# First block of a transformer kernel: modulated and projected in halves of 256 queries, with the first loads reordered and the later ones held back

## The chip, the cores and the metric

The kernel runs on one core of a Trainium2 chip. The metric is device time in microseconds (us) of one execution. Before the change it is 564.21 us, the median of 3 runs (564.14 to 564.25). All runs told here are of state "fast" (none is over 1.5% above the fastest of its kernel); comparisons are between runs of the same rounds on the same chip, unless it is said that runs of two groups are taken together.

## The reference

A layer norm with modulation from a vector c, grouped attention over the last 512 keys, a projection, and a second modulated norm with an MLP. Only the beginning matters here:

```python
mod = (_silu(c) @ w_mod).reshape(c.shape[0], 6, 1, -1)     # c: (1, 512), w_mod: (512, 3072)
sa, ca, ga, sb, cb, gb = ...
h = _layernorm(x) * (1 + ca) + sa                          # x: (1, 2048, 512), bf16
q = h @ wq                                                 # 32 heads of 128
scores = einsum('bhqd,bhkd->bhqk', q, k) * Dh ** -0.5      # k: last 512 rows of the cache
# ... softmax, @ v, @ wo; x + ga * A; second norm with sb, cb; MLP; x + gb * B
```

## The kernel before

Five engines work side by side: TensorE (PE; its weight loads are PEld), VectorE (DVE), ScalarE (ACT), GpSimd (POOL) and SyncE (SP), which here only issues loads. The 2048 queries go through in four blocks of 512. A block has four tiles of 128 rows (xn). They are normalised, transposed into hT (features on partitions), modulated on the way out of PSUM (the memory that TensorE writes to), and multiplied with wq one head at a time. The kernel starts with the loads; `eng=ACT` issues on ScalarE's queue, everything else on SyncE's:

```python
    for i in range(2):
        dma(x_sb[:, 2 * i:2 * i + 2, :], xv[:, 2 * i:2 * i + 2, :], f"xa{i}", writes=R_x[2 * i:2 * i + 2], eng=ACT if i else SP)
    dma(c_row[:, :], c[0].rearrange("(c p) -> c p", p=P), "c", writes=[R_c])
    load_wm01(0)            # first half of the modulation weights, 512 KB
    load_wm01(1, ACT)       # second half
    load_wq(0, 2, ACT)
    load_wq(2, 2)
    load_k(0)
    load_v(0)
    # ... constants
    warm(7)                 # 512-column matmuls on ones; their result is not used
    silu_exp(5)             # transposes c and takes its exp
    warm(9)
    # ... statistics of tile 3 on ACT
    ln_stat(0); ln_stat(1); rstd_add(0, 2); rstd_pow(0, 2)
    ln_stat(2); rstd_add(2, 3); rstd_pow(2, 4)
    silu_mul(5)             # rest of SiLU, on DVE
    for tl in range(3):
        ln_norm(tl)         # DVE
    # ... norm of tile 3 on ACT
    fs = mod_cols_mm(0, QBK)            # 32 one-column matmuls with wm0 and wm1
    # ... first half of fs, transposes of tile 0, second half of fs
    mod_cols_evac(0, QBK)
    for tl in range(1, TPB):
        ln_tposes(tl, [0, 2])
        warm(tl)
    ln_mod_ps([0, 2], hT[0], R_hT[0], 1)   # modulation, 512 columns a piece: two on DVE, two on ACT
    # ... further loads
    q_mms(0)
    q_mms(1, 5)
```

(Commands on one line are put together here; cuts are marked.)

## Time and profile before

| | before |
|---|---|
| time, span | 564.26, 562.5 us |
| x landed (two halves) | 4.78, 4.98 us |
| modulation weights landed (ACT half, SP half) | 6.16, 7.95 us |
| 32 modulation columns begin | 8.25 us |
| first modulation (hT) | 10.80 us |
| first score matmul | 13.47 us |

The rows below the first are from the start of the span and tell when each stage begins. PE is the bound for the rest of the span, so a change of the start is worth what it moves the first score matmul. The lines are in the prediction. The clock column of a stretch tells the granted TensorE clock as the trace's clock records have it; before the first record it reads 1.00, while the matmuls of that time take the 0.43 us of half speed. In this profile the record begins at 6.72.

### The profile page before, as it was taken

Reading aid. Unit: us, or ns where it says so; the run is one execution under the profiler, and the core shown is the slowest. Engines: PE = TensorE matmul, PEld = TensorE weight load, DVE = VectorE, ACT = ScalarE, POOL = GpSimd, SP = SyncE. Lnnn points to the kernel's source line nnn. Section 1 sums busy time; section 2 is a strip of 40 time slices with the busy share of each in tenths; the row PEclk is TensorE's granted clock in tenths of the full one; section 3 lists DMA queues with packets and bytes.
Section 4 is the critical chain, followed back from the end, with each engine's and each line's share of the span. In section 5 each row is a group of like instructions: output and inputs, shape, how many; then the busy total and the mean of one; then the engine's idle time right before and its main releaser. Section 6 shows DMA issues by size and latency. Waiting matters only on the chain.

```text
span 562.5 us, 9700 instructions
## 1 busy us (share of the span) xinstructions
PE 553.7 (98%) x4097; PEld 316.9 (56%) x4172; DVE 242.2 (43%) x533; ACT 350.4 (62%) x453; POOL 38.7 (7%) x42
## 2 busy tenths in 40 slices
PE   8999999999999999999999999999999999999998
PEld 3565555555555555555555555555555654444444
DVE  4444465533334655333346553333354448321134
ACT  5986666666666666666666666666666644432500
POOL 1000000003300000033000000330000000000000
PEclk9999999999999999999999999999999999999999
DMA  9778776421331247332523522121123220210001
GB/s 268 204 165 167 143 160 132 113 38 38 39 76 37 39 93 133 57 94 46 144 56 57 102 50 39 39 40 40 39 39 72 44 31 0 41 36 24 22 28 48
DMA packets 113310, 42.70 MB, mean 76 GB/s; under 512 B 93928, under 2 KB 112104, under 8 KB 113256
## 3 DMA queue, kind: packets, MB, share of 16 engines
q1 hardware_dynamic: 112024, 40.82, 35.2%
q10 hardware_dynamic: 1232, 1.15, 0.6%
q8 instruction: 35, 0.57, 0.5%
q14 instruction: 19, 0.16, 0.1%
HBM read 18.35 MB, written 2.10 MB: 36 GB/s over the span
## 4 chain that ended last, share of the span: by engine, by line
PE 97%; issue 1%; DMA 1%; DVE 1%
PE psS L1363 28%; PE psO L1363 26%; PE psQ L1363 23%; PE psW L1363 20%; DMA x<-in_A_x_dram 1%; DVE st L1373 0%; PE psS L1366 0%; DVE mv L1374 0%; DVE rstd L1574 0%; DVE PT L1673 0%; DVE PT L1675 0%; DVE tmp L1427 0%; DVE sc_bf L1428 0%; DVE tmp L1426 0%
## 5 line engine op out<-in xcount | busy, mean ns | idle before, releaser
L1482 ACT ACTIVATE PT<-psS 128x1024 bf16<-128x1024 f32 x256 | 262.6, 1028 | 129.5 <-PE psS L1363 129.4
L1363 PE MATMUL psS<-qT,kT 128*128 128x512 bf16 x509 | 151.1, 379 | 0.2
L1363 PEld LDWEIGHTS psO<-v,PT 128*128 128x128 bf16 x2048 | 126.6, 98 | 30.2
L1363 PE MATMUL psO<-v,PT 128*128 128x129 bf16 x2048 | 137.0, 220 | 0.0
L1363 PE MATMUL psQ<-hT,wq 128*128 128x512 bf16 x507 | 130.3, 379 | 0.1
L1492 DVE RECIPROCAL rinv<-psO 128x4 f32<-128x4 f32 x128 | 23.4, 183 | 233.1 <-PE psO L1363 233.1
L1363 PE MATMUL psW<-wo,oT 128*128 128x512 bf16 x451 | 117.9, 379 | 3.2
L1493 DVE TENSOR_TENSOR o<-psO,rinv 128x512 bf16<-128x512 f32 x128 | 88.5, 692 | 4.4
L1363 PEld LDWEIGHTS psQ<-hT,wq 128*128 128x128 bf16 x508 | 49.6, 98 | 60.7 <-issue 0.5
L1363 PEld LDWEIGHTS psS<-qT,kT 128*128 128x128 bf16 x512 | 49.6, 98 | 59.3 <-ACT PT L1482 0.7
L1474 ACT ACTIVATE qT<-psQ 128x512 bf16<-128x512 f32 x127 | 75.2, 592 | 0.5 <-PE psQ L1363 0.5
L1662 ACT ACTIVATE wq<-psS 128x512 bf16<-128x512 f32 x56 | 33.4, 597 | 49.6 <-PE psS L1363 49.6
L1363 PEld LDWEIGHTS psW<-wo,oT 128*128 128x128 bf16 x512 | 45.0, 98 | 32.9 <-DVE acc L1515 1.2
L1515 DVE TENSOR_TENSOR acc<-psW,acc 128x512 f32<-128x512 f32 x48 | 33.2, 691 | 6.7 <-PE psW L1363 6.7
L1363 PE MATMUL psO<-wmw,wq 128*128 128x512 bf16 (+1 forms) x164 | 32.7, 352 | 0.3
L1518 POOL TENSOR_TENSOR acc<-acc,gaf 128x512 f32<-128x512 f32 x12 | 15.3, 1272 | 168.7 <-DVE acc L1515 168.7
L1379 POOL TENSOR_TENSOR rstd<-rstd,cst 128x4 f32<-128x4 f32 x7 | 7.1, 1012 | 265.3 <-DVE rstd L1378 265.3
L1363 PE MATMUL psS<-h2T,wmw 128*128 128x512 bf16 x110 | 25.2, 379 | 0.1
L1673 DVE TENSOR_TENSOR PT<-psO,gbf 128x512 f32<-128x512 f32 (+1 forms) x12 | 7.5, 624 | 40.4 <-PE psO L1363 40.4
L1363 PEld LDWEIGHTS psO<-wmw,wq 128*128 128x128 bf16 x168 | 15.4, 98 | 16.5
L1363 PE MATMUL psS<-hT,wmw 128*128 128x512 bf16 x110 | 24.4, 379 | 0.1
L1373 DVE BATCH_NORM_STATS2 st<-x 128x6 f32<-128x512 bf16 x31 | 21.0, 678 | 4.8 <-DMA x<-in_A_x_dram 4.8
(73 smaller groups left out, 170.4 us busy)
## 6 DMA issues: line engine op xcount, KB each, us to landing
wo<-in_A_wo_dram SPq DMA_DIRECT2D x4, 1024.0 KB, 5.7
wq<-in_A_wq_dram SPq DMA_DIRECT2D x7, 512.0 KB, 5.7
wmw<-in_B_w_dram SPq DMA_DIRECT2D x14, 256.0 KB, 3.3
wmw<-in_w_mod_dram SPq DMA_DIRECT2D x5, 512.0 KB, 4.7
oT<-o SPq DMA_TRANSPOSE x128, 2.4
out_dram<-PT SPq DMA_DIRECT2D x15, 128.0 KB, 1.8
x<-in_A_x_dram SPq DMA_DIRECT2D x3, 512.0 KB, 4.1
v<-in_A_v_cache_dram SPq DMA_DIRECT2D x8, 128.0 KB, 4.8
```

What stands on the lines that cost most here:

```text
L1363: kb.op(PE, lambda e: e.matmul(out_ap, lhsT, rhs, start=start, stop=stop), reads=reads, group_writes=[R_b[k] for k in bk], signal=signal)
L1373: kb.op(DVE, lambda e: e.bn_stats(st[:, t, :], x_sb[:, t, :]), reads=[R_x[t]], writes=[R_st[t]])
L1379: kb.op(POOL, lambda e: e.tensor_tensor(rstd[:, sl], rstd[:, sl], cst[:, 0:1].to_broadcast([P, hi - lo]), op=ALU.pow), reads=R_rstd[sl] + ...
L1474: kb.op(ACT, lambda e: e.activation(qT[u % NQT][:, :], bank[bk], ACTF.Copy), reads=[R_b[bk]], writes=[R_qT[u % NQT]])
L1482: kb.op(ACT, lambda e: e.activation(PT[u % NPT][:, pr * 2:pr * 2 + 2, :], s_ps[pr][:, :, :], ACTF.Exp, scale=scale), reads=[R_b[pr * 2], R ...
L1492: kb.op(DVE, lambda e: e.reciprocal(rinv[:, u, :], o_ps[:, :, P]), reads=[R_b[5], R_b[6]], writes=[R_rinv])
L1493: kb.op(DVE, lambda e: e.tensor_tensor(o_sb[u % NOS][:, :, :], o_ps[:, :, 0:P], rinv[:, u, :].unsqueeze(2).to_broadcast([P, TPB, P]), op=A ...
L1515: kb.op(DVE, lambda e: e.tensor_tensor(acc[:, tl, :], bank[WBK], acc[:, tl, :], op=ALU.add), reads=[R_b[WBK], R_acc[tl]], writes=[R_acc[tl]])
L1518: kb.op(eng, lambda e: e.tensor_tensor(acc[:, tl, :], acc[:, tl, :], gaf[:, :], op=ALU.mult), reads=[R_acc[tl], R_ga], writes=[R_acc[tl]])
L1662: kb.op(ACT, lambda e: e.activation(h1T[b % 2][:, fc, :], bank[bk], ACTF.Relu), reads=[R_b[bk]], writes=[R_h1[b % 2][fc]], pre=all_events( ...
L1673: kb.op(DVE, lambda e: e.tensor_tensor(yt[i][:, c0:c1], bank[bk][:, c0:c1], gbf[:, c0:c1], op=ALU.mult), reads=[R_b[bk], R_gb], writes=[R_ ...
```

## The change

It wants to bring the first score matmul forward in four ways: the SiLU of c off the chain behind the statistics (c loaded first), fewer loads in flight until x has landed, tile 3 normalised on POOL, and the first block modulated and projected in two halves of 256 queries, so that the second half's norms and transposes lie beside the first half's modulation.

```diff
+    dma(c_row[:, :], c[0].rearrange("(c p) -> c p", p=P), "c", writes=[R_c], eng=ACT)
     for i in range(2):
         dma(x_sb[:, 2 * i:2 * i + 2, :], xv[:, 2 * i:2 * i + 2, :], f"xa{i}", writes=R_x[2 * i:2 * i + 2], eng=ACT if i else SP)
-    dma(c_row[:, :], c[0].rearrange("(c p) -> c p", p=P), "c", writes=[R_c])
     load_wm01(0)
     load_wm01(1, ACT)
-    load_wq(0, 2, ACT)
+    kb.op(SP, lambda e: e.nop(), reads=[R_x[0]])
+    load_wq(0, 2)
+    load_k(0)
     load_wq(2, 2)
-    load_k(0)
     load_v(0)
 ...
-    warm(7)
+    warm(6)
     silu_exp(5)
-    warm(9)
+    warm(8)
 ...
+    silu_mul(5)
     ln_stat(0)
 ...
-    silu_mul(5)
-    for tl in range(3):
-        ln_norm(tl)
- ...  (tile 3 on ACT)
+    ln_norm(0)
+    ln_norm(1)
+    kb.op(POOL, lambda e: e.tensor_scalar(xn[:, t3, :], x_sb[:, t3, :], s3[:, 1:2], rstd[:, t3:t3 + 1], op0=ALU.add, op1=ALU.mult), ...)
 ...
+    ln_tposes(0, TB[0])
+    ln_tposes(1, TB[0])
+    warm(1)
+    mod_half(0, 0, DVE)
+    mod_half(0, 2, ACT)
+    mod_half(0, 1, DVE)
+    mod_half(0, 3, ACT)
+    ln_norm(2)
+    q_half(0, 0, CC_ORDER[:3], QBK)
+    ln_tposes(3, TB[1])
+    ln_tposes(2, TB[1])
+    q_half(0, 0, CC_ORDER[3:], QBK)
+    mod_half(1, 0, DVE)
+    mod_half(1, 2, ACT)
+    mod_half(1, 1, DVE)
+    mod_half(1, 3, DVE)
+    q_half(1, 0, CC_ORDER, 5)
+    for u, bk in ((0, QBK), (1, 5)):
+        q_half(u, 1, CC_ORDER, bk)
+        q_evac(u, bk)
 ...
-    q_mms(0)
-    q_mms(1, 5)
```

More of the change, by code (lines that the diff above doesn't have):

```diff
@@ L1311, in build_fast @@
     R_st, R_mv, R_rstd = RL("st", NT), RL("mv", NT), RL("rstd", NT)
+    R_h0 = RL("h0", DC)
     R_s3, R_eps = Res("s3"), Res("eps")
@@ L1397, in ln_tposes @@
         for cc in range(DC):
-            bk = bks[cc // 2]
+            bk = bks[cc]
             o = (cc % 2) * 512 + tl * P
             tpose(bank[bk].bitcast(BF)[:, o:o + P], xn[:, tl, cc * P:(cc + 1) * P], [R_xn[tl]], [bk], cc == DC - 1)
-    def ln_mod_ps(bks, dst, R_dst, which):
-        o, r = (0, R_moda) if which == 1 else (2 * DC, R_modb)
-        for k in range(2):
-            for half, eng in ((0, DVE), (1, ACT)):
-                cc = half * 2 + k
-                src = bank[bks[half]].bitcast(BF)[:, k * 512:(k + 1) * 512]
-                sc, sh = modc[:, o + DC + cc:o + DC + cc + 1], modc[:, o + cc:o + cc + 1]
-                if eng is DVE:
-                    kb.op(DVE, lambda e, src=src, sc=sc, sh=sh, cc=cc: e.tensor_scalar(dst[:, cc, :], src, sc, sh, op0=ALU.mult, op1=ALU.add),
-                          reads=[R_b[bks[half]], r], writes=[R_dst[cc]])
-                else:
-                    kb.op(ACT, lambda e, src=src, sc=sc, sh=sh, cc=cc: e.activation(dst[:, cc, :], src, ACTF.Identity, bias=sh, scale=sc),
-                          reads=[R_b[bks[half]], r], writes=[R_dst[cc]])
     CC_ORDER = (0, 2, 1, 3)
@@ L1469, in q_mms, with q_evac @@
         b, h = units[u]
-        order = CC_ORDER if u < QA else range(DC)
-        for i, cc in enumerate(order):
+        for i, cc in enumerate(range(DC)):
             mm(bank[bk], wq_sb[:, cc, h * Dh:(h + 1) * Dh], hT[b % 2][:, cc, :], i == 0, i == DC - 1,
-               [R_wq[h], R_hT[b % 2][cc]], [bk], i == DC - 1)
+               [R_wq[h], R_hT[b % 2][cc]] + ([R_h0[cc]] if b == 0 else []), [bk], i == DC - 1)
+        q_evac(u, bk)
+    def q_evac(u, bk=QBK):
         kb.op(ACT, lambda e: e.activation(qT[u % NQT][:, :], bank[bk], ACTF.Copy), reads=[R_b[bk]], writes=[R_qT[u % NQT]])
@@ L1586, in build_fast @@
     rstd_pow(2, 4)
-    silu_mul(5)
-    for tl in range(3):
-        ln_norm(tl)
-    kb.op(ACT, lambda e: e.activation(s3[:, 3:4], s3[:, 1:2], ACTF.Copy, scale=rstd[:, t3:t3 + 1]), reads=[R_s3, R_rstd[t3]], writes=[R_s3])
-    kb.op(ACT, lambda e: e.activation(xn[:, t3, :], x_sb[:, t3, :], ACTF.Identity, scale=rstd[:, t3:t3 + 1], bias=s3[:, 3:4]),
-          reads=[R_x[t3], R_rstd[t3], R_s3], writes=[R_xn[t3]])
-    fs = mod_cols_mm(0, QBK)
-    for f in fs[:len(fs) // 2]:
-        f()
-    ln_tposes(0, [0, 2])
@@ L1597, in build_fast @@
-    for f in fs[len(fs) // 2:]:
+    ln_norm(0)
+    ln_norm(1)
+    kb.op(POOL, lambda e: e.tensor_scalar(xn[:, t3, :], x_sb[:, t3, :], s3[:, 1:2], rstd[:, t3:t3 + 1], op0=ALU.add, op1=ALU.mult),
+          reads=[R_x[t3], R_rstd[t3], R_s3], writes=[R_xn[t3]])
+    for f in mod_cols_mm(0, QBK):
         f()
     mod_cols_evac(0, QBK)
-    for tl in range(1, TPB):
-        ln_tposes(tl, [0, 2])
-        warm(tl)
-    ln_mod_ps([0, 2], hT[0], R_hT[0], 1)
+    HB = QB // 2
+    R_half = [R_h0, R_hT[0]]
@@ new lines, in build_fast, with mod_half @@
+    TB = [[0, 0, 2, 2], [1, 1, 3, 6]]
+    def mod_half(hf, cc, eng):
+        bk = TB[hf][cc]
+        o = (cc % 2) * 512 + hf * HB
+        src, dst = bank[bk].bitcast(BF)[:, o:o + HB], hT[0][:, cc, hf * HB:(hf + 1) * HB]
+        sc, sh = modc[:, DC + cc:DC + cc + 1], modc[:, cc:cc + 1]
+        if eng is DVE:
+            kb.op(DVE, lambda e: e.tensor_scalar(dst, src, sc, sh, op0=ALU.mult, op1=ALU.add), reads=[R_b[bk], R_moda], writes=[R_half[hf][cc]])
+        else:
+            kb.op(ACT, lambda e: e.activation(dst, src, ACTF.Identity, bias=sh, scale=sc), reads=[R_b[bk], R_moda], writes=[R_half[hf][cc]])
@@ new lines, in q_half @@
+    def q_half(u, hf, order, bk):
+        for cc in order:
+            mm(bank[bk][:, hf * HB:(hf + 1) * HB], wq_sb[:, cc, u * Dh:(u + 1) * Dh], hT[0][:, cc, hf * HB:(hf + 1) * HB], cc == CC_ORDER[0], cc == CC_ORDER[-1],
+               [R_wq[u], R_half[hf][cc]], [bk], cc == CC_ORDER[-1])
+    ln_tposes(0, TB[0])
[7 more added lines that the diff above has]
+    q_half(0, 0, CC_ORDER[:3], QBK)
@@ L1604, in build_fast @@
+    ln_tposes(3, TB[1])
[8 more added lines that the diff above has]
+        q_half(u, 1, CC_ORDER, bk)
+        q_evac(u, bk)
     load_wq(R, R)
```

## The prediction

> **What bounds the kernel now.** I read the page first: its busy shares, then its chain that ended last.
>
> ```profile
> span 562.5 us, 9700 instructions
> PE 553.7 (98%) x4097; PEld 316.9 (56%) x4172; DVE 242.2 (43%) x533; ACT 350.4 (62%) x453; POOL 38.7 (7%) x42
> ...
> PE 97%; issue 1%; DMA 1%; DVE 1%
> ```
>
> TensorE (PE) is busy 98% and is 97% of the chain. DMA, DVE and issue are 3% of the chain between them, and the change works only on those and on the matmuls just behind them. Next I cut the span into stretches (columns: stretch, length, busy us of each engine with its instructions, clock, DMA share, GB/s).
>
> ```profile
> 0.00:4.80 4.80, 3.44 (x9) 1.12 (x10) 0.00 (x1) 1.54 (x3) 1.02 (x9) 1.00 0.59 191
> ...
> 300.00:400.00 100.00, 99.21 (x786) 59.43 (x799) 42.87 (x99) 69.02 (x86) 11.74 (x10) 1.00 0.27 48
> ```
>
> From 300 to 400 us PE has under 1 us in 100 to give away, and the change leaves that work as it is. Whatever it brings must come from the start, before the first score matmul (psS<-qT,kT). PE is "busy" there too, but with matmuls on a tile of ones that only keep its clock up. So for the start I read the chain of waits, in order of time (start, length, what).
>
> ```profile
> 0.79 3.99 DMA x<-in_A_x_dram
> ...
> 4.80 0.70 DVE st L1373
> ...
> 7.71 0.09 DVE tmp L1426
> ...
> 7.82 0.19 DVE tmp L1427
> ...
> 8.03 0.17 DVE sc_bf L1428
> ...
> 8.25 0.55 PE psQ L1363 x16
> ...
> 10.11 0.43 PE psW L1363 x2
> 10.54 0.22 PE psS L1366 x4
> ```
>
> The reader is to see three stages. Until 4.80 all wait for the first half of x. From there to 8.2 DVE does the statistics of three tiles and then the SiLU of c (tmp, sc_bf), which the modulation matmuls wait for. From 8.25 PE does modulation columns, transposes and, in between, clock-keeping matmuls. The timeline has the end of the start (start, length, engine, operation, what ended the idle time).
>
> ```profile
> 10.80 1.45 ACT L1413 ACTIVATE hT<-psS,modc 128x512 bf16<-128x512 bf16 x2 [1.08 <-PE psS L1366]
> 10.80 1.00 DVE L1410 TENSOR_SCALAR hT<-psS,modc 128x512 bf16<-128x512 bf16 x2 [0.98 <-PE psS L1366]
> ...
> 12.73 0.60 ACT L1474 ACTIVATE qT<-psQ 128x512 bf16<-128x512 f32 x1 [0.48 <-PE psQ L1363]
> ...
> 13.47 0.59 PE L1363 MATMUL psS<-qT,kT 128*128 128x512 bf16 x2
> ```
>
> The first score matmul is at 13.47. If later work only shifts, the time changes by as much as this number does. Last, the DMA issues of the first 3 us (size, us from issue to landing):
>
> ```profile
> wmw<-in_w_mod_dram SPq DMA_DIRECT2D x1, 512.0 KB, 6.3
> wq<-in_A_wq_dram ACTq DMA_DIRECT2D x1, 256.0 KB, 7.4
> ...
> kT<-in_A_k_cache_dram SPq DMA_TRANSPOSE x1, 7.2
> ```
>
> With issue times 1.65, 1.71 and 2.62 from the timeline, they land at 7.95, 9.1 and 9.8. The wq half is not used before 11.5, kT not before 13.4: both are early by some us, which lets them be held back.
>
> **What the Trainium skill says.**
> - "DMA: Bandwidth & Descriptors", section "Issuing engines are not separate DMA queues": transfers from different issuers run on the same 16 DMA engines and interleave; "Queues, rings and completion order" adds that each engine takes turns between queues. The trace agrees in part: between 3 and 4.5 us the ACT queue takes 79% and the SP queue 23% of the engines. But in that stretch only 40 packets are under 2 KB: x and the modulation weights have 2 KB rows, wq has 512-byte rows. So wq, kT and v, which the change holds back, had hardly begun when x landed. What still shares with x is what the change leaves in flight.
> - "TensorE: Matmul & The Clock Gate", section "The HAM clock gate": half clock until about 3.4 us of sustained activity. The trace agrees: 512-column matmuls issue every 0.43 us until 6.7 and every 0.22 afterwards.
> - "GPSIMD Engine Reference", section "Elementwise — side-by-side cycle accounting": a tight loop takes 769 ns for 512 elements, two-input operations more. No row here is a one-input POOL operation of that size; the two-input one (acc times gaf, 128x512) takes 1272 ns. My estimate for the new POOL operation is 0.95 us, between them.
> - "VectorE: DVE Perf Modes", section "The perf-mode tier table": a tensor_scalar that reads PSUM reaches at most twice the basic rate. The two modulations start 0.46 us apart for 512 columns, under the 0.53 that one element per cycle at its 0.96 GHz would need, so that rate is in use.
>
> **The change part by part.** I rebuild the start with durations from this trace, and with the new instruction order and waits from the built program.
>
> *1. SiLU ahead of the statistics; c first on the ACT queue.* c leaves at 0.78 instead of 1.24, with no x in front of it in its queue. It should land by 3 instead of 4.5. Six clock-keeping matmuls of 0.43 from 1.04 end at 3.6, then the transpose of c (0.18), exp (0.17) and three DVE operations (pitch 0.2) end near 4.6. So 0.49 us (7.62 to 8.11) leaves the DVE chain behind the statistics and lies in time in which DVE idled. DVE is free for the statistics from about 4.55.
>
> *2. Less in flight.* x's first half goes alone for about 0.4 us, because c delays the second. By the packet sizes the rest buys little. I choose a landing at 4.4 (before: 4.8), so the statistics start at S = 4.55, 0.25 earlier. The second half lands at about 4.9 as before; its first DVE use is S + 1.8 = 6.4, so it is in time.
>
> *3. Norms and modulation columns.* From the statistics' start to the end of the last rstd addition is 2.9 us (4.80 to 7.70). Then two norms (pitch 0.32, last one 0.41) end at S + 3.55 = 8.1. PE does its eight clock-keeping matmuls (3.75 to about 7.0), then the 32 modulation columns (16 take 0.38 to 0.55) once both weight halves have landed. The SP half is issued 0.45 earlier with no wq behind it: 7.0 to 7.3. So they end near 8.0, where they used to begin at 8.25. The DVE copies of the columns (2 x 0.2) end near 8.45; transposes of tiles 0 and 1 end (0.22 each and 0.2 to drain) near 8.6. The first modulation starts at T = 8.65, not 10.80.
>
> *4. Halves.* A 256-column modulation: from 4 and 512 columns (162 and 542 ns on DVE) about 0.35; on ACT from 1 and 512 columns (294 and 773 ns) about 0.53. Half 0, two each: DVE done at 9.3, ACT at 9.65. The norm of tile 2 follows on DVE, 9.65. POOL: power 7.5 to 8.25, then tile 3 until 9.2. PE: three query matmuls of 0.11 behind the modulations, tile 3 from 9.45, tile 2 from 9.7, drained at 10.15. Half 1: DVE does three in a row, 10.15 to 11.1; ACT's one is hidden. The last query matmul and drain (0.3) end at 11.4, the copy (0.6) at 12.0, the score matmul follows 0.15 later: 12.15 to 12.3.
>
> So 13.47 becomes about 12.25, a gain of 1.2 us. Two 256-wide operations cost more than one 512-wide one (0.70 against 0.54 on DVE), and three serial ones sit on the path; but they replace 1.45 us on ACT, and two clock-keeping matmuls (0.43 at 10.11) and the third tile leave the path.
>
> *5. What is held back.* SP waits for x (4.4), then issues wq (0.5), kT (1.2 to 1.8), the other wq and v. Weights drain until about 6.5, wq (256 KB at the 340 GB/s of this stretch: 0.8) lands near 7.7, needed at 9.0; kT near 9.5, needed at 12.2; the second wq near 10.7, needed at 12.7. All in time, the tightest by 1.3 us.
>
> *Sum:* 564.21 - 1.2 = 563.0 us, 0.2% less.
>
> **The rivals.**
> - *The held-back loads become the wait.* For it: kT took 7.2 us to land; at 5.0 + 7.2 = 12.2 it would be exactly on the edge. Against: its 7.2 had 1.5 MB in front of it; here most of that is gone by 6.5. If true, the gain shrinks to 0 to 0.8: 563.4 to 564.2.
> - *POOL or DVE sets the end.* If tile 3 takes 1.6 us on POOL rather than 0.95, its transposes move to 9.9 and the gain falls by 0.2; beyond that one for one. ACT's old version ended at 9.72. Time: 563.2 to 563.6.
> - *The clock.* PE has more gaps between 8.6 and 12 than before (two fillers are gone). A return to half speed for one window would cost about 1 to 2 us: 564 to 565. Against: my estimate still has PE busy some 65% there.
> - *x lands much earlier.* Then SiLU, not x, starts the statistics at 4.55, so no more than 0.1 comes of it.
> - *The gain is swallowed later.* ACT is busy 11.2 of the 11.6 us after 13.44, but that work begins with the first scores, so it shifts too. I see no fixed-time event behind it.
>
> **Range and chances.** The clear terms are SiLU and the fillers (0.5 and 0.4); the landing of x, POOL's time and the DMA edge each leave 0.2 to 0.5 open. I take 562.5 to 563.8. For 2% the time would have to change by 11.3 us, near the length of the whole start, so "within 2%" is almost certain: 0.98, with 0.01 each for the others.
>
> **What would show it.** Right: exp of c before 4.2 and sc_bf before x's first statistics; x landing 4.2 to 4.6; first hT at 8.4 to 8.9; first score matmul at 12.1 to 12.5; PE waits of no DMA after x but perhaps w_mod; the stretch from 300 to 400 unchanged. Wrong: PE waiting for wq or kT; POOL's tile 3 over 1.3 us; 512-column matmuls 0.43 apart after 8 us; or a first score matmul that moved by more or less than the total did.

## The result and the profile after

The changed kernel takes 565.35 us (median of 6 runs, 563.86 to 566.50); the kernel before took 564.12 in the same rounds (6 runs). The ratio is 1.0021, with a 95% interval of 1.0007 to 1.0036: within 2%, but slower, and above the predicted range of 562.5 to 563.8. A ratio here is the mean time of one kernel's runs over that of the other's of the same rounds, so it is not quite the ratio of the medians.

The page of the changed kernel, span, busy shares and chain:

```profile
span 563.1 us, 9781 instructions
PE 557.5 (99%) x4173; PEld 318.0 (56%) x4173; DVE 243.0 (43%) x536; ACT 349.5 (62%) x452; POOL 39.4 (7%) x43
...
PE 98%; DMA 1%; DVE 0%; ACTq 0%; issue 0%; ACT 0%
```

PE is the bound as before. The page alone hides where the time went: a busier PE looks better. (PE's records went from 4097 to 4173: the trace of before lacks some matmuls, so its 98% is a little low.) The chain of waits of the changed kernel's start (start, length, what):

```profile
0.79 0.56 ACTq L1298
...
1.39 0.37 ACTq L1298
...
1.79 6.37 DMA wmw<-in_w_mod_dram
...
8.21 0.90 PE psQ L1364 x30
...
9.62 0.42 DVE hT L1595
```

Before, the chain went through x, the statistics and SiLU. Now it goes through one load: the second half of the modulation weights (wmw), issued at 1.79 as third on ACT's queue and landed at 8.16. Statistics, norms and SiLU are off the chain, as intended, but what took their place is nearly as late: the columns begin at 8.21, where they began at 8.25. The timeline at the same places (start, length, engine, what; in brackets the idle time and what ended it):

```profile
4.63 0.68 DVE L1374 BATCH_NORM_STATS2 st<-x 128x6 f32<-128x512 bf16 x1
...
6.28 0.63 ACT L1558 ACTIVATE xn<-x 128x512 bf16<-128x512 bf16 x1 [2.17 <-DMA x<-in_A_x_dram]
...
8.21 0.90 PE L1364 MATMUL psQ<-sc_bf,wmw 128*128 128x1 bf16 x30 [1.13 <-DMA wmw<-in_w_mod_dram]
...
9.37 0.77 POOL L1580 TENSOR_SCALAR xn<-x,s,rstd 128x512 bf16<-128x512 bf16 x1
...
14.20 0.59 PE L1364 MATMUL psS<-qT,kT 128*128 128x512 bf16 x2 [0.34 <-ACT qT L1463]
```

PE idles 1.13 us for the weights, ACT 2.17 us for the second half of x. The first modulation is at 9.62 (before 10.80), 1.2 us earlier, yet the first score matmul comes at 14.20 (before 13.47). So between them the changed kernel needs 4.58 us where my prediction had 3.6. The stretches tell why. Columns are stretch, length, busy us of PE, PEld, DVE, ACT and POOL, clock, DMA share, GB/s; after, then before:

```profile
6.12:9.53 3.41, 2.23 (x45) 1.48 (x42) 2.25 (x9) 2.04 (x6) 1.57 (x3) 1.00 1.25 260
9.53:12.94 3.41, 3.16 (x20) 2.21 (x19) 2.12 (x7) 1.59 (x3) 0.61 (x1) 0.50 1.20 297
12.94:16.36 3.42, 3.08 (x18) 1.41 (x16) 0.31 (x1) 2.62 (x5) 0.00 (x0) 1.00 1.12 330
300.00:400.00 100.00, 100.00 (x808) 59.66 (x806) 43.54 (x101) 69.44 (x87) 11.73 (x10) 1.00 0.28 50
```

```profile
6.72:10.13 3.41, 2.88 (x50) 1.97 (x50) 2.62 (x11) 1.48 (x4) 1.48 (x2) 1.00 1.30 248
10.13:13.54 3.41, 3.33 (x18) 1.31 (x17) 1.33 (x3) 2.04 (x3) 0.00 (x0) 1.00 1.16 322
```

From 9.53 to 12.94, exactly in the tail of transposes and query matmuls, the granted clock is 0.50; before, it stays at 1.00. "PE busy 3.16" is not work done there: the same matmuls take twice as long. After 12.94 both run at full speed, and from 300 to 400 us nothing has changed. Last, the loads (size, us from issue to landing), after and then before:

```profile
wmw<-in_w_mod_dram SPq DMA_DIRECT2D x1, 512.0 KB, 5.5
wmw<-in_w_mod_dram ACTq DMA_DIRECT2D x1, 512.0 KB, 6.4
x<-in_A_x_dram SPq DMA_DIRECT2D x1, 256.0 KB, 3.2
x<-in_A_x_dram ACTq DMA_DIRECT2D x1, 256.0 KB, 4.9
```

```profile
wmw<-in_w_mod_dram ACTq DMA_DIRECT2D x1, 512.0 KB, 4.9
x<-in_A_x_dram ACTq DMA_DIRECT2D x1, 256.0 KB, 4.2
x<-in_A_x_dram SPq DMA_DIRECT2D x1, 256.0 KB, 4.0
```

With issue times from the timeline the first half of x lands at 4.01 instead of 4.78, but the second, issued at 1.39 behind c (whose issue alone took 0.56 us), at 6.25 instead of 4.98. Its queue had stood still. From 3.0 to 3.5 us the queues moved (q1 is SyncE's, q10 ScalarE's; packets, MB, share of the 16 engines), after and then before:

```profile
q1 hardware_dynamic: 59, 0.10, 80.2%
```

```profile
q1 hardware_dynamic: 43, 0.08, 51.4%
q10 hardware_dynamic: 46, 0.09, 48.3%
```

After, q10 has no line there: c's packets pass at 1.74 to 1.80, and the first packet of the x behind c follows only at 3.58 (before, with x first in that queue, at 2.01). Then x shares the DMA engines with the first half of the weights, which was issued 0.15 us before it on SyncE's queue and landed at 6.75. The other half of the weights stood third behind c and x and came last. Its end was slow: from 7.0 to 7.5 us its queue moved ten packets, beside 352 of SyncE's, where wq and kT were under way (issued from 4.11 on, as soon as the first half of x had landed):

```profile
q1 hardware_dynamic: 352, 0.15, 106.9%
q10 hardware_dynamic: 10, 0.02, 9.6%
```

### The profile page after: what moved, and what is told of

It is laid out like the page before. It is cut to its first block, busy times and chain, and to the rows that moved or that the text cites. A ratio compares the mean times of both kernels' runs of the same rounds, so it can differ in the third digit from the quotient of the medians.

```text
span 563.1 us, 9781 instructions
## 1 busy us (share of the span) xinstructions
PE 557.5 (99%) x4173; PEld 318.0 (56%) x4173; DVE 243.0 (43%) x536; ACT 349.5 (62%) x452; POOL 39.4 (7%) x43
## 4 chain that ended last, share of the span: by engine, by line
PE 98%; DMA 1%; DVE 0%; ACTq 0%; issue 0%; ACT 0%
PE psS L1364 28%; PE psO L1364 26%; PE psQ L1364 23%; PE psW L1364 20%; DMA wmw<-in_w_mod_dram 1%; PE psS L1367 0%; ACTq L1298 0%; ACT qT L1463 0%; DVE hT L1595 0%; DVE PT L1691 0%; DVE PT L1693 0%; PE psO L1367 0%
## 5 line engine op out<-in xcount | busy, mean ns | idle before, releaser
L1364 PE MATMUL psQ<-hT,wq 128*128 128x512 bf16 (+1 forms) x512 | 131.3, 379 | 0.3 <-DVE hT L1595 0.3
L1364 PE MATMUL psW<-wo,oT 128*128 128x512 bf16 x512 | 130.6, 379 | 0.0
```

What stands on the lines that cost most here:

```text
L1364: kb.op(PE, lambda e: e.matmul(out_ap, lhsT, rhs, start=start, stop=stop), reads=reads, group_writes=[R_b[k] for k in bk], signal=signal)
```

## The experiments

*Theory:* the new order of issue makes the last modulation weights late; PE idles for them; and so little work in that stretch lets the clock fall to half speed for a stretch of 3.41 us. *Rivals:* (a) the halves themselves cost more than they save; (b) the held-back loads or the wait on SyncE cost the time; (c) the half-speed stretch is chance and has nothing to do with the change.

Twelve kernels ran, in four groups, each with its own runs of the kernel before on the same chip. All gave correct results. A mean clock of 0.997 is one half-speed stretch in a run (half of 3.41 us in 563 is 0.3%), 0.994 is two (0.001 less where the clock also falls in the last microsecond, as in the first profile); this is how unprofiled runs are sorted below. "Outside" is time minus span, the median of the runs.

| kernel | median us (n) | before, same group | ratio, 95% interval | runs at 0.997 or less | outside |
|---|---|---|---|---|---|
| changed kernel, first rounds | 565.35 (6) | 564.12 | 1.0021 [1.0007, 1.0036] | 5 of 6 | 1.91 |
| e1_fill | 564.63 (5) | 564.07 | 1.0005 [0.9991, 1.0018] | 1 of 5 | 1.91 |
| e2_xfirst | 564.73 (6) | 564.07 | 1.0008 [0.9994, 1.0022] | 2 of 6 | 1.99 |
| e3_nohold | 566.92 (4) | 564.07 | 1.0052 [1.0032, 1.0072] | 4 of 4 | 1.76 |
| e4_halves | 563.90 (5) | 564.07 | 0.9991 [0.9978, 1.0004] | 0 of 5 | 1.72 |
| e5_loads | 564.62 (5) | 563.82 | 1.0016 [1.0003, 1.0030] | 1 of 5 | 1.89 |
| e6_xfirst_fill | 563.68 (5) | 563.82 | 0.9996 [0.9982, 1.0009] | 0 of 5 | 1.98 |
| e7_hold | 564.25 (5) | 563.82 | 1.0005 [0.9992, 1.0019] | 0 of 5 | 2.05 |
| e8_idle | 565.87 (5) | 563.82 | 1.0031 [1.0018, 1.0045] | 5 of 5 | 1.77 |
| e9_nonop | 563.91 (5) | 563.95 | 0.9999 [0.9985, 1.0012] | 1 of 5 | 1.80 |
| e10_best | 563.75 (5) | 563.95 | 1.0005 [0.9991, 1.0019] | 0 of 5 | 1.82 |
| e11_again | 564.49 (6) | 564.00 | 1.0009 [0.9989, 1.0028] | 3 of 6 | 1.93 |
| e12_fill_nonop | 564.19 (5) | 564.00 | 1.0004 [0.9991, 1.0016] | 1 of 5 | 1.75 |

The kernel before had none at 0.997 or less in its 40 runs of these groups, and 1.74 to 1.77 us outside.

### e1_fill: keep PE busy until the weights land

```diff
     silu_exp(5)
-    warm(8)
+    warm(13)
```

> The changed kernel with 13 instead of 8 clock-keeping matmuls ahead of the modulation columns, so that TensorE does not idle while it waits for the second half of the modulation weights (it idled from 7.08 to 8.21 us). Theory 1 (the loss is a clock window: the idle stretch makes the throttle grant half speed from 9.5 to 12.9 us): no half-speed window, clock 1.000 in nearly all runs, first score matmul near 13.1 instead of 14.2, time 563.5 to 563.9 with a spread of under 0.3 us, as the one run of the changed kernel at clock 1.000 (563.86). Theory 2 (the loss is the late weights alone, the clock is a by-product): the weights still land at about 8.2, so the time stays at 565 to 566.

The half-speed stretch was gone in 4 of 5 runs, and the median fell to 564.63, but not to the 563.5 to 563.9 that I had hoped for. In its profile the second half of the weights still landed at 8.25. From the first modulation (9.71) to the first score matmul (13.47) it needed 3.76 us instead of 4.58. The chain of waits of its start shows what it paid with:

```profile
1.04 2.74 PE psW L1364 x6
...
3.90 4.38 PE psW L1364 x13
```

The thirteen fillers, most of them still at half speed (the clock record begins at 6.83), took 4.38 us and ended at 8.28, just as the weights landed, so the chain runs through them and they cost next to nothing here (first modulation at 9.71, before them 9.62). With a clock that comes up still later they would be the wait, as in the profile of e4 below. The clock part of the theory held; the late weights stayed.

### e2_xfirst: both halves of x ahead of the weights

```diff
-    dma(c_row..., eng=ACT)
+    dma(c_row...)                       # SP, then x's first half, then the first weights
 ...
-    load_wm01(1, ACT)                   # third on ACT
+    load_wm01(1, ACT)                   # second on ACT, right after x's second half
```

> The changed kernel with the loads issued in another order: c, then the first half of x on SP; the second half of x alone on ACT at once, and ACT's half of the modulation weights only after the dummy exponential (about 2.7 us). Theory 1 (the DMA engines serve the loads nearly in order of issue over both queues, so what is issued ahead of x delays it): second half of x lands at 4.0 to 4.6 instead of 6.25, first half at 4.4 to 4.9 instead of 4.0, both weight halves by 7.4 instead of 8.2; TensorE waits for weights under 0.4 us; first modulation at 8.6 to 9.0 instead of 9.62; without a half-speed window the score matmul at 12.3 to 12.7 and the time near 563.0 to 563.4. Theory 2 (landing is set by sharing, not by order): x's second half and the weights land within 0.4 us of where they did, and so does the time.

The loads of its first 2 us:

```profile
wmw<-in_w_mod_dram ACTq DMA_DIRECT2D x1, 512.0 KB, 5.7
wmw<-in_w_mod_dram SPq DMA_DIRECT2D x1, 512.0 KB, 6.1
x<-in_A_x_dram ACTq DMA_DIRECT2D x1, 256.0 KB, 3.2
x<-in_A_x_dram SPq DMA_DIRECT2D x1, 256.0 KB, 3.4
```

Issued at 0.79 and 1.22, x landed at 3.96 and 4.62; the weights, issued at 1.27 and 1.65, at 6.93 and 7.77. So the order of the loads decides who lands when. Two things were changed at once, though: c no longer stood ahead of x's second half, and the weights no longer went out before it; the run does not tell which of them mattered more. (The new place of ACT's weights, behind a dummy exponential, delayed nothing: they were issued at 1.27 and not at the 2.7 of my expectation.) My expectation for the last weights (7.4 or earlier) was missed, and with it those for the first modulation (9.35) and the score matmul: x and these weights are 1.5 MB together, and in all kernels that hold wq back the last of it landed at 7.4 to 8.3, whatever the order. The columns began at 7.91 and the first score matmul at 13.08, but PE still idled 1.99 us before them, and 2 of 6 runs had the half-speed stretch.

### e3_nohold: no wait for x before the later loads

```diff
     load_wm01(1, ACT)
-    kb.op(SP, lambda e: e.nop(), reads=[R_x[0]])
     load_wq(0, 2)
```

> The changed kernel without the wait of the SP queue for x: wq, kT and v are issued at once. Theory 1 (order of issue rules): x's first half still lands at 4.0 (within 0.2), its second half at 6.3 and the weights at 8.2 (within 0.4); wq and kT land earlier; time as the changed kernel, 565 to 566. Theory 2 (holding back is what frees x): x's first half lands at 4.5 or later and the weights at 9 or later, time over 566.

This went against what I had written: I thought that holding back bought almost nothing. The timeline:

```profile
9.91 0.93 PE L1364 MATMUL psQ<-sc_bf,wmw 128*128 128x1 bf16 x30 [2.65 <-DMA wmw<-in_w_mod_dram]
...
16.12 0.59 PE L1364 MATMUL psS<-qT,kT 128*128 128x512 bf16 x2 [0.34 <-ACT qT L1463]
```

The first half of x landed at 4.01 as with the wait, but the second at 7.75 instead of 6.25, although wq and kT were issued behind it: what comes later on the other queue takes its share too, and strict order of issue (theory 1) is wrong there. And SyncE now issued wq at 1.71, before ACT got to the last weights at 1.78, and these landed at 9.86 instead of 8.16. PE idled 2.65 us, and all four runs had a half-speed stretch. So the wait does nothing for x's first half; it protects its second half and the modulation weights, and in this order of issue is worth 1.7 us of their landing (one profile each). Rival (b) falls in so far as not holding back is worse still. Whether a later release, on the weights instead of x, would have spared the slow end of the weights was not run. Longer idling went with more half-speed stretches, which speaks against (c).

### e4_halves: the halves with the loads, fillers and SiLU of before

```diff
-  # loads of the changed kernel; warm(6), warm(8); silu_mul before ln_stat(0)
+  # loads of the kernel before; warm(7), warm(9); silu_mul after rstd_pow(2, 4)
```

> The kernel before in its loads, its clock-keeping matmuls and its place of the SiLU (behind the statistics), with the halves, the new transpose order and the third tile on POOL kept from the changed kernel. Theory 1 (halves help, the new loads hurt): the modulation columns start at 8.25 as before, first modulation at 9.6 to 9.8, score matmul at 12.9 to 13.2 at full clock, time 563.5 to 563.9; a half-speed window in few runs or none, since TensorE does not idle over a microsecond. Theory 2 (the halves themselves, with their gaps on TensorE, bring the half-speed window): clock below 1.000 in most runs and time 565 or more.

No run lost its clock, and 563.90 against 564.07 is no slower than before: rival (a) falls. In its profiled run the clock came up only at 9.33, the nine fillers took 3.95 us and became the wait (the weights had landed at 7.93), and the columns began at 8.76; from the first modulation (10.29) to the first score matmul (14.01) it needed 3.72 us. That tail is what I had predicted as 3.6.

### e5_loads: the kernel before with the new loads alone

```diff
-  # loads of the kernel before
+  # loads of the changed kernel, with the wait for x
```

> The kernel before with nothing but the changed kernel's loads: c first on ACT, x's second half behind it, SP waiting for x before it issues wq, kT and v. Theory 1 (the new order of issue is what hurts): x's second half lands at 6.2 to 6.8 instead of 5.0 and ACT's half of the weights at about 8.2 instead of 6.2; the third tile's norm on ACT ends near 11.0 instead of 9.72, the first modulation starts near 11.5 instead of 10.80, the score matmul near 14.1, time 564.7 to 565.3. Theory 2 (the loads are harmless, the halves or the SiLU order hurt): score matmul within 0.2 of 13.47 and time within 0.2 of the kernel before.

564.62 against 563.82: the loads alone make the kernel before 0.16% slower. The second half of x landed at 6.61 and the last weights at 8.14; since tile 3 still is normalised on ACT, the late x pushed the first modulation to 11.28 and the first score matmul to 13.94. One of five runs fell to half speed.

### e6_xfirst_fill: order of e2 with fillers

```diff
   # on top of e2
-    warm(8)
+    warm(11)
 ...
-    warm(1)
+    warm(2)
```

> The changed kernel with the loads of the run that issues x ahead of the weights, and more clock-keeping matmuls: 11 instead of 8 ahead of the modulation columns, 2 instead of 1 ahead of the first query matmul. Theory 1 (two separate losses, late weights and the clock window): clock 1.000 in all runs, columns at 7.8 to 8.0, score matmul at 12.9 to 13.2, time 563.6 to 564.0, so 0.1 to 0.5 under the kernel before. Theory 2 (fillers cost what they save, or the window comes anyway): a clock under 1.000 in two runs of five or more, time 564.4 or more.

No half-speed run, and 563.68 against 563.82. In the profile the columns begin at 7.88 and the first score matmul comes at 13.06, as in e2. So with both causes mended at once the loss is gone, but hardly a gain is left. One reason is outside the span: 1.98 us against 1.75.

### e7_hold: the kernel before, with the wait for x alone

```diff
     load_wm01(1, ACT)
-    load_wq(0, 2, ACT)
-    load_wq(2, 2)
+    kb.op(SP, lambda e: e.nop(), reads=[R_x[0]])
+    load_wq(0, 2)
     load_k(0)
+    load_wq(2, 2)
```

> The kernel before with only the holding back: x, c and the weights issued as before, SP waiting for x before wq, kT and v. Theory 1 (what is issued behind x does not slow x): x lands at 4.8 and 5.0 as before (within 0.2), SP's half of the weights 0.2 to 0.7 earlier than 7.95, wq and kT in time, score matmul at 13.3 to 13.5, time within 0.2 of the kernel before. Theory 2 (holding back frees x): x lands 0.4 or more earlier. A side question: with the wait on SP three kernels took 1.9 us outside the span instead of 1.7; if the wait causes that, this kernel shows 1.9 too.

Two lines of its timeline:

```profile
4.48 0.69 DVE L1373 BATCH_NORM_STATS2 st<-x 128x6 f32<-128x512 bf16 x1 [4.48 <-DMA x<-in_A_x_dram]
...
13.15 0.59 PE L1363 MATMUL psS<-qT,kT 128*128 128x512 bf16 x2
```

The statistics start 0.32 us earlier than before (4.80), and so does the first score matmul (13.47). That looks like the gain that holding back was meant to bring, but it is one profile each, and among the profiles of kernels with the changed kernel's loads and the wait the first half of x lands anywhere from 4.01 to 4.45: not shown. The last weights came at 7.38 instead of 7.95, as theory 1 said. The time shows no gain: 564.25, with 2.05 us outside the span instead of 1.75.

### e8_idle: the kernel before with four fillers fewer

```diff
     silu_exp(5)
-    warm(9)
+    warm(5)
```

> The kernel before with 5 instead of 9 clock-keeping matmuls ahead of the modulation columns, so that TensorE idles for about 1.5 us before them; nothing else differs. Theory 1 (an idle stretch of about a microsecond in an otherwise thin window is enough for half speed): a half-speed window of 3.4 us in most runs, clock 0.997, score matmul at 14.0 to 14.8, time 565.0 to 565.8. Theory 2 (the half-speed window of the changed kernel comes from its halves, not from idling): clock 1.000 and the time within 0.2 of the kernel before.

Nothing but idling is added here: loads and halves are those of before. Its stretches:

```profile
3.87:7.29 3.42, 1.60 (x7) 0.50 (x6) 2.40 (x6) 2.10 (x7) 0.52 (x1) 1.00 1.06 374
7.29:10.70 3.41, 2.26 (x44) 2.21 (x46) 2.04 (x10) 1.11 (x2) 0.95 (x2) 0.50 1.28 248
10.70:14.11 3.41, 3.41 (x14) 1.50 (x12) 1.33 (x3) 1.45 (x2) 0.00 (x0) 0.50 1.16 321
14.11:17.52 3.41, 3.41 (x17) 1.32 (x15) 0.00 (x0) 2.48 (x4) 0.00 (x0) 1.00 1.16 314
```

PE idles 2.17 us before its columns, and two half-speed stretches follow. All five runs show one or two, and the kernel is 0.31% slower. That shows that idling PE is enough: rival (c) falls, in so far as it denies any tie to the work. Chance still has a part, as the repeat below shows.

### e9_nonop: the wait as part of the load

```diff
   # on top of e6
-    kb.op(SP, lambda e: e.nop(), reads=[R_x[0]])
-    load_wq(0, 2)
+    load_wq(0, 2, after=[R_x[0].w])     # the same wait, attached to the load
```

> The run with x ahead of the weights and the extra clock-keeping matmuls, but SP's empty instruction that waits for x is gone: the wq load itself waits for x. The landings stay as they were (x 3.8 and 4.4, weights 7.3 and 7.75), score matmul near 13.05, span 561.6 to 562.3. Theory 1 (the empty instruction costs the 0.2 to 0.3 us that all kernels with it spend outside the span): time less span falls from 1.9 to 2.1 to 1.75, time 563.3 to 563.6. Theory 2 (the later loads, not the instruction, cause it): time less span stays at 1.9 or more.

Outside the span it takes 1.80 us instead of 1.98. The span gained nothing. In the profiled run the last weights landed at 8.13 and PE idled 1.86 us; the clock stretch that ended at 10.72 had little work in it, and the next was at half speed. It is the one run of five that fell.

### e10_best: halves, before's order of loads, attached wait, more fillers

```diff
   # the changed kernel with
+  # x on both queues first, then c (SP) and the weights; the wait attached to the wq load
+  # warm(7), warm(11), warm(2); silu_mul after rstd_pow(0, 2)
```

> A version meant to beat both kernels: halves as in the changed kernel; loads in the old order of issue with wq, kT and v held until x has landed (the wait in the load itself); SiLU on DVE after the first rstd addition; 11 clock-keeping matmuls ahead of the columns. Theory 1 (weights and clock were the losses): x at 4.5 and 4.6, weights at 6.0 and 7.4, columns start at 7.4 to 7.7, first modulation at 8.9 to 9.2, score matmul at 12.6 to 13.0, clock 1.000 in all runs, time 563.1 to 563.5, so 0.3 to 0.7 under the kernel before. Rival (DVE sets the end: SiLU is back in its chain): first modulation at 9.3 or later and time as the previous best, 563.5 to 563.9.

Two lines of its timeline:

```profile
7.54 0.94 PE L1364 MATMUL psQ<-sc_bf,wmw 128*128 128x1 bf16 x32 [0.27 <-DMA wmw<-in_w_mod_dram]
...
12.86 0.59 PE L1364 MATMUL psS<-qT,kT 128*128 128x512 bf16 x2 [0.34 <-ACT qT L1463]
```

Here the last weights land at 7.41, the earliest with the halves, and the first score matmul comes at 12.86, which is 0.61 us earlier than before. That is about half of the 1.2 us that I had predicted. The first modulation, at 9.14, came as theory 1 said; the median, 563.75, did not, and lies where the rival had it. The runs scatter from 563.32 to 565.07 though none lost its clock, so the ratio is 1.0005 with an interval that holds 1. None of the versions beats the kernel before by more than the runs can tell. The kernel before scatters alike (563.58 to 565.10 on another chip, at full clock). In the profiles that have a clock record it begins at anything from 3.75 to 9.33 us, so this is a likely cause, but unprofiled runs do not record it: it is argued, not shown.

### e11_again and e12_fill_nonop: the changed kernel once more, and with fillers and the attached wait

```diff
   # e11: no edit;  e12, on top of the changed kernel:
-    warm(8)
+    warm(13)
 ...
-    kb.op(SP, lambda e: e.nop(), reads=[R_x[0]])
-    load_wq(0, 2)
+    load_wq(0, 2, after=[R_x[0].w])
```

> The changed kernel once more, unedited, on the same chip as the next run. Theory (late weights, then a half-speed clock window, then the wait instruction on SyncE): the median is 564.9 to 565.7, at least three of five runs or more show a mean clock of 0.997 or less, and time outside the span is 1.85 to 2.0 us. Rival (the half-speed windows of the first six runs were that chip's or that hour's): clock 1.0 in nearly all runs and a median of 563.9 to 564.3.

> The changed kernel with thirteen instead of eight clock-keeping matmuls and the wait for x attached to the first query-weight load instead of an instruction of its own. Theory: no half-speed window in at least four of five runs (0.7 to 0.9 us less in those), 0.1 to 0.25 us less outside the span (1.75 to 1.8): median 564.2 to 564.6, 0.7 to 1.1 us under the unedited changed kernel, but still no faster than the kernel before by more than 0.2, because the weights land at 8.1 to 8.3 as before. Rival (the window is only a by-product and the late weights alone set the time): within 0.3 us of the unedited changed kernel.

The unedited changed kernel was better this time: 564.49, below the range I gave, with three of six runs that fell. It scattered from 563.33 to 566.64, and the runs sort by clock: 563.33, 563.43 and 564.19 at full clock; 564.79 and 565.75 with one half-speed stretch; 566.64 with two. The profile fell on a run at full clock:

```profile
7.93 0.90 PE L1364 MATMUL psQ<-sc_bf,wmw 128*128 128x1 bf16 x30 [1.35 <-DMA wmw<-in_w_mod_dram]
...
13.21 0.59 PE L1364 MATMUL psS<-qT,kT 128*128 128x512 bf16 x2 [0.34 <-ACT qT L1463]
```

PE idles for the weights as in the first profile (1.35 us), but the clock stretches lie otherwise: they run from 4.12 to 7.53 and on to 10.95, so the idle time falls on two of them rather than in the middle of one, and both keep full clock. So the same kernel loses its clock or keeps it, and where the stretches fall is the difference that these two profiles show.

e12 removed the 0.18 us outside the span (1.75) and had one half-speed run of five, as the theory said. Its median, 564.19, is only 0.30 us under e11's, where I expected 0.7 to 1.1: the median does not tell the theory from its rival here. One reason can be read from e11: half of its runs had kept their clock and were the fastest. Whether the fillers cost something is open: e12's four runs at full clock average 564.12, e11's three 563.65, but they run from 563.41 to 564.74, and in e12's profile PE still waits 0.47 us for the weights behind them.

## Why the prediction was wrong, by its own steps

**The second half of x and the weights (steps 2 and 3, the term that failed first).** Step 2 let c delay x's second half by about 0.4 us and had it land "at about 4.9 as before"; it came at 6.25. c cost its queue much more than its issue time: the first packet of the x behind it moved at 3.58 instead of 2.01, and then it shared the engines with weights issued before it. (The same standstill would explain why the first half of x came at 4.01, earlier than the 4.4 of the prediction.) The trace of before had a sign of it: SyncE's weights, issued at 1.65 behind c, began only at 4.80, after half a microsecond in which that queue moved no data; the prediction read that queue's 23% as sharing alone. Step 3 gave a time for SyncE's half of the weights only, "7.0 to 7.3"; that half was even earlier, 6.75. ScalarE's half, landed at 6.16 before, has no line in the prediction: behind c and x in its queue it came last, at 8.16, with its last packets beside the held-back wq and kT (step 5 had them behind it). How much of the delay is c, the other weights or wq was not separated. In the changed kernel this made the columns begin at 8.21, and the first modulation come at 9.62 rather than 8.65: 1.0 us of the 1.2 that I had promised.

**The clock (a rival that I argued away).** I gave it "1 to 2 us: 564 to 565" and then set it aside because PE would be busy 65% between 8.6 and 12. I looked in the wrong place. (Its "the trace agrees" was generous too: the two rates are there, but full speed came 5.7 us after the first filler, not 3.4.) What mattered was the stretch before, in which PE waited for the weights and then did one-column matmuls. My estimate of how much of a full-clock stretch is spent streaming columns, from the starts of the matmuls in the trace and 0.22 us for 512 columns (double before the clock comes up), gives:

| full-clock stretch | columns stream | next stretch |
|---|---|---|
| e3, 6.90 to 10.31 | 10% | half |
| e8, 3.87 to 7.29 | 37% | half |
| changed kernel, 6.12 to 9.53 | 37% | half |
| e9, 7.31 to 10.72 | 39% | half |
| e11, 7.53 to 10.95 | 39% | full |
| e5, 5.79 to 9.20 | 44% | full |
| e11, 4.12 to 7.53 | 50% | full |
| before, 6.72 to 10.13 | 52% | full |

So 44% and more kept full clock, 37% and less lost it, and 39% did either; in every other run with a clock record, the first full-clock stretch has over 50% and kept it. This is an estimate with a margin: counted from the ends of the matmuls, which the trace models, single values move by up to 5 points and e11's lowest (34%) falls below e8's (39%). Whether the throttle counts columns at all is not shown. PE's busy time does not sort them: 2.23 us of the changed kernel's stretch and 2.25 of e5's are on different sides, and e11's first has only 1.94. One-column matmuls are many and busy, but stream almost nothing. The kernel before has a margin; the changed one is in the doubtful range, and the position of the stretches, which differed between two profiles of the same kernel (ends at 6.12 and 9.53, at 4.12 and 7.53), can decide.

What it costs: the two profiles of the changed kernel need 4.58 and 3.87 us from the first modulation to the first score matmul, so 0.7 us there. Sorted by clock, its twelve runs, of two groups, average 563.70 at full clock (4 runs), 565.25 with one half-speed stretch (5), and 566.36 with two (3): 1.5 us for the first (1.4 and 1.6 within the two groups). Half of 3.41 us, 1.7, is the most that one can cost if PE is the bound all through. Why the runs differ by more than the two profiles is open; the unprofiled ones do not record where the stretch lay.

**Outside the span (not in the prediction).** The wait on SyncE as an instruction of its own goes with 0.14 to 0.3 us outside the span: medians of 1.89 to 2.05 in all kernels that have it, 1.72 to 1.82 in those that have not (before, e3, e4, e8) or have it attached to the load (e9, e10, e12). By what mechanism is open.

**The sum.** Predicted were 563.0 us. The late weights add about 1.0, the wait outside the span 0.2, and a half-speed stretch 0.7 to 1.5 in the 8 of 12 runs that have one or two: about 565 for the usual run and 564.2 for a run at full clock, against 565.35 and 563.7 measured. So the estimate is rough by about half a microsecond.

**What was right.** SiLU left the chain: statistics at 4.63 (predicted 4.55). Earlier x brought no more than that, as one rival said: its first half landed at 4.01, before DVE had begun with SiLU (4.14). Two norms ended 3.55 us after the statistics began, as predicted (its terms, 2.9, 0.32 and 0.41, add up to 3.63). POOL's tile 3 took 0.77 us (predicted 0.95). The halves' tail at full clock took 3.72 to 3.87 us (predicted 3.6). The held-back loads came in time: no wait for wq or kT appears. And the stretch from 300 to 400 us did not change. At full clock the changed kernel averages 563.70, inside the predicted range, but that is luck in part: three of the four runs are of a chip where single runs of the kernel before took 563.58 to 565.10, and in the profile at full clock the first score matmul came at 13.21, a gain of 0.26 us and not of 1.2.

## What to carry to other kernels

When work is taken off a chain, ask first which load becomes the last wait, and look at what stands in front of it in its own queue, a load of 1 KB too, and at what shares the DMA engines with it from the others. Before accepting an idle gap of PE near the start, count the columns that stream in any 3.4 us around it, not the instructions or the busy time (this rests on the estimate above); a kernel with few of them shows scattered times, so sort its runs by granted clock before comparing. Fillers are a remedy only as long as they end before the data land, even at half speed.

## What the Trainium skill lacked or had wrong

- "TensorE: Matmul & The Clock Gate", section "The HAM clock gate": it puts the return to half clock after "≥1 idle window (~3.4µs)". The window length agrees (the half-speed stretches last 3.41 us, or twice that). It does not say how little work makes a window idle: here PE was not idle throughout, idle times of 1.1 to 2.7 us sufficed in some runs, where columns streamed in 39% of the window or less (my estimate). The page gives no such share.
- "DMA: Bandwidth & Descriptors" does not give what a small load costs the load behind it in its queue. The first packet of x moved 1.0 to 1.3 us after its issue where x was first in its queue, 1.5 to 1.6 us after it behind c (1 KB) on SyncE's queue (e2, e6, e9), and 1.9 to 2.3 us after it behind c on ScalarE's (the changed kernel twice, e1, e3, e5, e12). By what mechanism is open.
- No page that I read has the cost of a wait on SyncE outside the span: 0.14 to 0.3 us as an instruction of its own, at most 0.05 when attached to a load (1.75 to 1.82 us against 1.74 to 1.77).
